# Attention feeding a four-expert layer on one core: units of queries cut to the chunks, the last chunk's tokens in a row, and one early product

## The chip, the cores and the metric

The kernel runs on one core of a Trainium2 chip. The metric is device time in microseconds (us), and lower is better. In three runs before the change it took 488.66, 488.98 and 489.07 us; the median, 488.98 us, is the time before.

A core has five engines that run their own instruction streams and wait for each other through semaphores: TensorE (PE in the profile, with its weight loads shown apart as PEld), VectorE (DVE), ScalarE (ACT), GpSimd (POOL) and SyncE (SP), which here only issues transfers.

## What is computed

Two blocks in a row. The first is attention whose weights are products of two small projections; the second sends every token through four experts and adds their outputs with normalised weights. Cut to what matters:

```
q, k, v: (4 batches, 4 heads, 1088 tokens, 32)     S1, S2: (8, 32)
phi(x)[i, j] = (S1 x)[i] * (S2 x)[j]               # 64 numbers for each token and head
kv = sum over tokens of phi(k) v^T                 # over all 1088 tokens of a batch and head
z  = sum over tokens of phi(k)
x  = (phi(q) kv) / (phi(q) z + 1e-6)               # token by token
x  -> (4352 tokens, 128)                           # batch, token; head and dim
p  = domain_probs / (sum + 1e-9)                   # (4352, 4)
out = sum over e of p[:, e] * (relu(x w1[e]) w2[e])    # w1: (4, 128, 1024), w2: (4, 1024, 128)
```

Everything is in float32. A token's output depends on the keys and values of its whole batch but on its own query only, so queries can be taken in any order.

## The kernel before

**Chunks and steps.** The expert layer is the bulk of the work. Its 4352 token columns are cut into 11 chunks (`CHUNKS`, line 67): 128, 448, 512, five of 512, 320, 256 and 128. `START` (line 69) has the first column of each. A chunk runs in 16 steps, four for each expert; a step takes 256 of the 1024 hidden features. `first` makes the step's hidden values: TensorE multiplies `xT` (tokens as columns) by `w1` into a PSUM bank named `h`, of which there are three, ScalarE applies relu (line 807), and VectorE makes the rectified differences that a fast form of the second product needs (line 778). `second` multiplies them into the output banks `o0` and `o1`. The loop at the end issues `first(i)` and then `second(i - LA)` with LA = 2, so that the two steps between hide ScalarE and VectorE. Every matmul goes through `on_side` (line 194), alternating between two halves of TensorE; `both` calls it twice. At the end of an expert `gather` copies the banks (ScalarE) and adds them with the token weights (GpSimd).

The first and the last chunk are `plain`: 128 columns, one `h` bank for a step, tokens on partitions in the output, and no differences. For the first three steps of chunk 0 the first 64 columns are multiplied ahead (`begun_hp`, `half_columns`), because half of `xT` is ready earlier than the other.

**Attention in pieces.** Attention runs inside the steps of the expert layer. `front` yields it in pieces, each with an instruction or a few: for batches 1 to 3 first `keys` (19 pieces, of which 3 turn the keys, 3 project them, 8 are products on VectorE, and two sums on TensorE), then `queries` for each unit of queries (20 pieces; the first of all has 18). A unit is a run of query columns; `UNITS` (line 65) gives the three units of each batch. The last piece of a unit sends its result through DRAM into `xT` and raises `have`. Batch 0's keys and first unit are written out in `start`.

**Pacing.** `needed` (lines 955 to 962) holds, for each chunk, how many pieces must be done for its last column, which is the count at the end of the unit that contains that column. At every step the loop takes, over all later chunks, the largest ratio of (pieces needed + 8 - pieces done) to columns left until the chunk starts, times the columns of a step; that is `rate`, pieces per step. `work`, called twice in a step, adds half of it to a credit and runs a piece for each whole credit. In the first two steps of chunk 1 nothing is added.

**The order of tokens.** VectorE turns 32 x 32 blocks, and the columns of a batch are laid so that a row of `qn` holds 34 neighbouring tokens (G = 34) of one head. So a column stands for every 34th token, and the last chunk of 128 columns holds 32 groups of 4 tokens, 34 apart. Its token weights (`ends`, line 149) and its output (line 851) follow that pattern: 32 rows of 4 x 128 numbers, 2 KB each, while the tile `end` has 128 partitions of 512 bytes.

**The start.** `start` (lines 666 and on) is one dependent chain: keys of batch 0, their products `kp` (line 383, shared between VectorE and GpSimd), the sums on TensorE (`f`), `key_divide` (`kvz`, line 406), the first 128 queries, and then chunk 0.

Of the kernel before, what the change touches and what calls it, by code (L numbers as in the profile page):

```python
# [23 lines left out]
def kernel(  # L24
# [20 lines left out]

    nc = tc.nc

    P = 128  # L50
# [11 lines left out]
    CW = 512  # L62
    GE = 160
    LA = 2
    UNITS = [[P, 448, 512]] + [[384, 384, 320]] * 2 + [[384, 320, 384]]

    CHUNKS = [P, 448, 512] + [512] * 5 + [320, 256, P]
    NC = len(CHUNKS)
# [14 lines left out]
    def psum(pool, tag):  # L83
        return pool.tile([P, 512], F32, tag=tag, name=tag)


    def load_rows(src, b, name, part=slice(0, S)):

        d = kn if name == "kn" else qn
        if b not in d:  # L90
            d[b] = lpool.tile([P, S], F32, tag=name, bufs=2, name=name)
        c, n = part.start, part.stop - part.start
        nc.sync.dma_start(d[b][:, part], bass.AP(src.tensor, src.offset + b * H * S * D + c, [[G * D, P], [1, n]]))  # L93

    def load_v(b):
        t = lpool.tile([P, H * NT * D], F32, tag="vn", name="vn")
# [29 lines left out]
    def load_w2(e):  # L126
# [14 lines left out]
    e_sum = cpool.tile([P, 2, 3], F32, name="e_sum")  # L141
    load_rows(q, 0, "qn", slice(P, S))
    load_w1(0)
    nc.sync.dma_start(
        dp.rearrange("p g e -> p (g e)"), bass.AP(domain_probs.tensor, domain_probs.offset, [[G * E, P], [1, G * E]])
    )
    for i, t in enumerate((0, (B - 1) * S + G - 4)):
        nc.sync.dma_start(
            ends[:, i, :], bass.AP(domain_probs.tensor, domain_probs.offset + t * E, [[G * E, 32], [1, 4 * E]])
        )  # L150
    load_w2(0)
    for e in range(1, E):
# [513 lines left out]
    def start():  # L666


        b, n = 0, UNITS[0][0]
        kf = []  # L670
        for t0 in (0, 2):
            key_turn(b, 0, t0, 2)
        for r in (1, 2):
            key_turn(b, r)
        qT = query_turn(b, 0, n)
        for gi in range(3):
            kf.append(psum(ps_h, "h"))
        value = value_copy(b)
        key_project(b, 0, kf[0])
        key_project(b, 1, kf[1])  # L680
        next(value)
        key_project(b, 2, kf[2])
        for _ in value:
            pass
        fq = [psum(ps_o, "o0"), psum(ps_o, "o1"), psum(ps_n, "num")]
        for i in range(3):
            for j in range(2):
                both(fq[i][:, 0:n], sr[:, i, j, :], qT[:, 0:n], start=(j == 0), stop=(j == 1))
        qb = apool.tile([P, QW], F32, tag="qb", name="qb")
        nc.scalar.copy(qb[:, 0:n], fq[0][:, 0:n])  # L690
        for x in range(2):
            key_product(b, 0, 4, 0, x, nc.vector, kf[0])
            key_product(b, 0, 4, 1, x, nc.gpsimd)
        for x in range(2):
            key_product(b, 4, 4, 0, x, nc.vector, kf[1])
            key_product(b, 8, 1, 0, x, nc.vector, kf[2])
        key_product(b, 4, 5, 1, 0, nc.gpsimd)
        key_product(b, 4, 4, 1, 1, nc.vector, kf[1])
        key_product(b, 8, 1, 1, 1, nc.vector, kf[2])
        kv = psum(ps_f, "f")  # L700
        for t0, n0 in ((0, 4), (4, 5)):
            for p in range(2):
                key_sum(b, p, kv, t0, n0)
        qp = query_tiles()
        for x in range(2):
            for p in range(2):
                query_product(qp, p, x, n, fq[1 + x], qb)
        for h in range(H):
            nc.gpsimd.tensor_copy(_ap(sq, 32 * h, 32, 32 * h, [[R2, 2], [1, R2]]), _ap(s_T, 0, 32, 0, [[D, 2], [1, R2]]))

        n1 = UNITS[b][1]
        qT = apool.tile([P, QW], F32, tag="qT2", name="qT2")
        turns = query_turns(b, n, n1, qT)
        next(turns)
        key_divide(b, kv)
        for _ in turns:
            pass
        first = attend_first(b, 0, n, qp)
        next(first)
        early[b, n] = psum(ps_o, "o1")  # L720
        both(early[b, n][:, 0:n1], sq[:, :], qT[:, 0:n1], start=True, stop=True)
        for _ in first:
            pass
        key_blocks(b, kv)
        gate_sums()
# [24 lines left out]
    def by_blocks(t, n, off=0):  # L750
        return _ap(t, 0, P, off, [[32, n // 32], [1, 32]])

    begun_hp = {}

    def half_columns(i, hp, c):

# [10 lines left out]
    def first(i, work):  # L767

        m, kq = steps[i]
        n, (e, f) = CHUNKS[m], divmod(kq, NP)
        w = n // 2
        hd = mpool.tile([P, 4 * CW], F32, tag="hid", bufs=4, name="hid")
        hid[i] = hd

        def rectify_and_subtract(out, src, in1):
            nc.vector.scalar_tensor_tensor(out=out, in0=src, scalar=0.0, in1=in1, op0=ALU.max, op1=ALU.subtract)  # L778

        if plain(m):  # L780
            if i in begun_hp:
                hp = begun_hp.pop(i)
                half_columns(i, hp, HP)
            else:
                hp = psum(ps_h, "h")
                for j in range(2):
                    both(
                        hp[:, n * j : n * j + n],
                        w1_sb[:, e, P * (2 * f + j) : P * (2 * f + j + 1)],
                        xT[:, START[m] : START[m] + n],  # L790
                        start=True,
                        stop=True,
                    )
            if m and kq % 2:
                nc.vector.tensor_scalar(
                    out=hd[:, 0 : 2 * n], in0=hp[:, 0 : 2 * n], scalar1=0.0, scalar2=None, op0=ALU.max
                )
            else:
                nc.scalar.activation(hd[:, 0 : 2 * n], hp[:, 0 : 2 * n], ACTF.Relu)  # L799
            work()  # L800
            work()
            return
        for j in range(2):
            hp = psum(ps_h, "h")
            c = P * (2 * f + j)
            both(hp[:, 0:n], w1_sb[:, e, c : c + P], xT[:, START[m] : START[m] + n], start=True, stop=True)
            nc.scalar.activation(hd[:, n * j : n * j + n], hp[:, 0:n], ACTF.Relu)  # L807
            if j == 0:
                rectify_and_subtract(hd[:, 4 * w : 5 * w], hp[:, w:n], hd[:, 0:w])
            else:  # L810
                rectify_and_subtract(
                    _ap(hd, 0, P, 5 * w, [[w, 2], [1, w]]),
                    _ap(hp, 0, P, w, [[0, 2], [1, w]]),
                    _ap(hd, 0, P, w, [[3 * w, 2], [1, w]]),
                )
                rectify_and_subtract(hd[:, 7 * w : 8 * w], hp[:, 0:w], hd[:, 6 * w : 7 * w])
            work()
# [3 lines left out]
    def second(i):  # L821
# [3 lines left out]
        if plain(m):  # L825

            if f == 0:
                acc[m] = psum(ps_o, f"o{e % 2}")
            for j in range(2):
                for _ in range(2):  # L830
                    on_side(
                        lambda s: acc[m][half[s], 0:DM],
                        lambda s: hd[:, n * j + HP * s : n * j + HP * s + HP],
                        lambda s: w2_sb[:, e, 2 * f + j, :],
                        start=(f == j == 0),
                        stop=(f == NP - 1 and j == 1),
                    )
            if f == NP - 1:
                p_e = ends[:, 1 if m else 0, e : e + 1]
                if e == 0:  # L840
                    total[m] = mpool.tile([P, P], F32, tag="end", name="end")
                    nc.vector.tensor_scalar(
                        out=total[m][:, :], in0=acc[m][:, 0:DM], scalar1=p_e, scalar2=None, op0=ALU.mult
                    )
                else:
                    nc.vector.scalar_tensor_tensor(  # L846
                        out=total[m][:, :], in0=acc[m][:, 0:DM], scalar=p_e, in1=total[m][:, :], op0=ALU.mult, op1=ALU.add
                    )
                if e == E - 1:
                    t = (START[m] // S) * S + START[m] % S // 32  # L850
                    nc.sync.dma_start(
                        bass.AP(out.tensor, out.offset + t * DM, [[G * DM, 32], [1, 4 * DM]]), total.pop(m)[:, :]
                    )
            return
        if f == 0:
            acc[m, e] = [psum(ps_o, "o0"), psum(ps_o, "o1")]
# [28 lines left out]
    def turn_back(m, src):  # L885
# [4 lines left out]
        for b, c, nn, at in parts(m):  # L890
            for a in range(4):
                nc.sync.dma_start(
                    bass.AP(
                        out.tensor,
                        out.offset + (b * S + c // 32) * DM + 32 * a,
                        [[G * DM, 32], [DM, nn // 32], [1, 32]],
                    ),
                    _ap(ob, 32 * a, 32, at, [[32, nn // 32], [1, 32]]),
                )
# [68 lines left out]
    for i in range(len(steps) + LA):  # L968
        if i < len(steps):
# [27 lines left out]
                load_batch(1)  # L997
            if m > 1 and kq == LA + 3 and m + 2 < NC:
                load_gate(m + 1)
        if i >= LA:  # L1000
            second(i - LA)
            mm, kk = steps[i - LA]
# [33 lines left out]
```

## Time and profile before

| | busy, us | instructions |
|---|---|---|
| PE, TensorE matmuls | 481.8 | 4543 |
| PEld, weight loads | 369.0 | 4543 |
| DVE, VectorE | 321.0 | 754 |
| ACT, ScalarE | 246.7 | 496 |
| POOL, GpSimd | 230.0 | 269 |

The profiled span is 487.2 us, the granted TensorE clock 0.999. Busy times of matmuls overlap, since two halves of the array run at once; the pace of TensorE is read from the starts of matmuls. Some rows that matter around the change:

| group | count | mean of one, ns |
|---|---|---|
| VectorE `hid`, line 778, 128x256 | 208 | 424 |
| VectorE `hid`, line 778, 128x512 | 96 | 686 |
| VectorE `hid`, line 778, 128x224 | 32 | 389 |
| VectorE `hid`, line 778, 128x448 | 16 | 616 |
| VectorE `kp`, line 383, 128x256 | 12 | 560 |
| VectorE `kp`, line 383, 128x320 | 12 | 709 |
| VectorE `kp` from `h`, line 383, 128x64 | 3 | 219 |
| VectorE `qp`, line 493, 64x384 | 24 | 793 |
| VectorE `qp`, line 493, 64x512 | 4 | 780 |

Transfers are busy for 19% of the 16 engines' time over the span, most of it in the first tenth, when the weights and the first two batches arrive.

### The profile page before, as it was taken

What the parts mean: (1) busy time and instruction counts of PE and PEld (TensorE: products, weight loads), DVE (VectorE), ACT (ScalarE), POOL (GpSimd) and SP (SyncE); (2) the same over time, 40 slices, a digit from 0 to 9 for tenths busy, and PEclk for the clock granted to TensorE, in tenths of its full rate; (3) what the DMA queues carried; (4) which work ended last, traced back from release to release, by engine and by line L of the source; (5) the groups of instructions that cost most, each with busy time, mean ns of one, the idle gap of its engine ahead of it and who ended that gap; (6) DMA issues with size and microseconds to landing.
All of it is one profiled execution on the core that took longest, in us unless ns stands there. A gap on an engine that the chain in (4) does not pass through costs nothing.

```text
span 487.2 us, 11354 instructions
## 1 busy us (share of the span) xinstructions
PE 481.8 (99%) x4543; PEld 369.0 (76%) x4543; DVE 321.0 (66%) x754; ACT 246.7 (51%) x496; POOL 230.0 (47%) x269
## 2 busy tenths in 40 slices
PE   8999999999999999999999999999999999999997
PEld 6966767677777777777777777777777777999997
DVE  6858685968776757768675674576574576665642
ACT  4354553445454634545455554545455555566751
POOL 5172653516354444425455354334555345565570
PEclk9999999999999999999999999999999999999999
DMA  8890230040103520041102200021101200120000
GB/s 238 259 299 11 90 93 2 22 116 1 35 1 100 123 53 1 1 118 24 34 1 86 50 2 2 1 86 24 34 0 56 50 1 0 45 54 4 15 3 18
DMA packets 37588, 26.25 MB, mean 54 GB/s; under 512 B 26016, under 2 KB 34592, under 8 KB 37024
## 3 DMA queue, kind: packets, MB, share of 16 engines
q1 hardware_dynamic: 37520, 25.53, 19.2%
q8 instruction: 36, 0.59, 0.5%
q14 instruction: 16, 0.13, 0.1%
q10 hardware_dynamic: 16, 0.00, 0.0%
HBM read 21.28 MB, written 4.24 MB: 52 GB/s over the span
## 4 chain that ended last, share of the span: by engine, by line
PE 95%; DVE 2%; DMA 1%; SPq 1%; issue 0%; ACT 0%; ACTq 0%
PE h L194 49%; PE o L194 40%; PE f L194 3%; PE den L194 2%; DMA vn<-in_v_dram 1%; DVE kp L383 1%; DVE hid L778 1%; SPq L99 0%; PE num L194 0%; DVE qp L493 0%; SPq L93 0%; ACT hid L807 0%; SPq L119 0%; DVE qT L480 0%; DVE end L846 0%
## 5 line engine op out<-in xcount | busy, mean ns | idle before, releaser
L194 PE MATMUL h<-xT,w_sb 128*64 128x512 f32 (+5 forms) x1432 | 299.5, 490 | 0.3 <-DVE hid L778 0.3
L778 DVE SCALAR_TENSOR_TENSOR hid<-h,hid 128x256 f32<-128x256 f32 (+6 forms) x432 | 203.8, 472 | 144.2 <-ACT hid L807 135.2
L807 ACT ACTIVATE hid<-h 128x512 f32<-128x512 f32 (+3 forms) x288 | 158.3, 550 | 193.8 <-PE h L194 154.1
L194 PE MATMUL o<-hid,w2s 128*64 128x256 f32 (+3 forms) x1152 | 222.8, 355 | 0.0
L194 PEld LDWEIGHTS h<-xT,w_sb 128*64 128x64 f32 x1432 | 148.8, 137 | 48.9 <-issue 4.1
L194 PE MATMUL o<-hid,w_sb 128*64 128x256 f32 (+3 forms) x864 | 184.1, 355 | 0.0
L194 PEld LDWEIGHTS o<-hid,w2s 128*64 128x64 f32 x1152 | 132.0, 137 | 29.4 <-issue 1.0
L922 POOL TENSOR_TENSOR ev<-yz,sh 64x256 f32<-64x256 f32 (+3 forms) x72 | 48.0, 667 | 161.7 <-ACT sh L925 159.0
L194 PEld LDWEIGHTS o<-hid,w_sb 128*64 128x64 f32 x864 | 100.8, 137 | 20.8 <-issue 2.1
L910 POOL TENSOR_TENSOR yz<-ev 128x512 f32<-128x512 f32 (+3 forms) x36 | 42.5, 1180 | 59.2 <-ACT ev L913 59.1
L922 POOL TENSOR_TENSOR ct<-ev 128x512 f32<-128x512 f32 (+3 forms) x36 | 42.0, 1167 | 2.8
L922 POOL TENSOR_TENSOR total<-total,ct 128x512 f32<-128x512 f32 (+3 forms) x27 | 32.4, 1200 | 2.1
L922 POOL TENSOR_TENSOR ct<-ct,gate 128x512 f32<-128x512 f32 (+3 forms) x27 | 32.2, 1191 | 2.1
L493 DVE TENSOR_TENSOR qp<-qa,qb 64x384 f32<-64x384 f32 (+3 forms) x44 | 31.9, 724 | 1.1
L912 ACT COPY ev<-o 128x512 f32<-128x512 f32 (+3 forms) x36 | 19.4, 538 | 12.0 <-PE o L194 11.5
L194 PE MATMUL o<-w_sb,hid 128*64 128x128 f32 x256 | 21.3, 274 | 0.0
L913 ACT COPY ev<-o 128x512 f32<-128x512 f32 (+3 forms) x36 | 19.4, 538 | 2.4 <-PE o L194 0.4
L194 PEld LDWEIGHTS o<-w_sb,hid 128*64 128x64 f32 x256 | 16.9, 137 | 1.8 <-issue 0.9
L799 ACT ACTIVATE hid<-h 128x256 f32<-128x256 f32 x24 | 8.8, 384 | 18.3 <-PE h L194 17.8
L383 DVE TENSOR_TENSOR kp<-fs 128x256 f32<-128x256 f32 (+1 forms) x24 | 15.1, 635 | 0.1
L194 PEld LDWEIGHTS den<-kvx,qp 128*64 128x64 f32 x264 | 13.1, 137 | 2.2 <-issue 0.2
L925 ACT COPY sh<-yz 64x256 f32<-64x256 f32 (+3 forms) x36 | 13.7, 379 | 1.6 <-POOL yz L910 0.8
(126 smaller groups left out, 239.3 us busy)
## 6 DMA issues: line engine op xcount, KB each, us to landing
w_sb<-in_moe_w_dram SPq DMA_DIRECT2D x8, 512.0 KB, 7.7
gate<-gates SPq DMA_DIRECT2D x4, 1024.0 KB, 4.8
kn<-in_k_dram SPq DMA_DIRECT2D x4, 544.0 KB, 4.3
vn<-in_v_dram SPq DMA_DIRECT2D x16, 128.0 KB, 4.5
gate<-gates SPq DMA_DIRECT2D x2, 896.0 KB, 4.5
qn<-in_q_dram SPq DMA_DIRECT2D x3, 544.0 KB, 5.7
xd<-y SPq DMA_DIRECT2D x26, 48.0 KB, 1.7
out_dram<-ob SPq DMA_DIRECT2D x16, 64.0 KB, 2.0
```

What stands on the lines that cost most here:

```text
L194: nc.tensor.matmul(out(s), weights(s), moving(s), **flags)
L383: eng.tensor_tensor(out=_ap(kps[b], 0, P, 256 * t0 + P * p + 64 * x, [[256, n], [32, 2], [R, 4], [1, R]]), in0=_ap(src, 0, P, off + 4 * x, ...
L493: nc.vector.tensor_tensor(out=qp[p][64 * x : 64 * x + 64, 0:n], in0=qa[64 * p : 64 * p + 64, 0:n], in1=qb[64 * p : 64 * p + 64, 0:n], op=A ...
L778: nc.vector.scalar_tensor_tensor(out=out, in0=src, scalar=0.0, in1=in1, op0=ALU.max, op1=ALU.subtract)
L799: nc.scalar.activation(hd[:, 0 : 2 * n], hp[:, 0 : 2 * n], ACTF.Relu)
L807: nc.scalar.activation(hd[:, n * j : n * j + n], hp[:, 0:n], ACTF.Relu)
L910: add = lambda out, in0, in1, op=ALU.add: nc.gpsimd.tensor_tensor(out=out, in0=in0, in1=in1, op=op)
L912: nc.scalar.copy(_ap(ev, 0, P, 0, [[2 * w, 2], [1, w]]), _ap(a0, 0, P, 0, two))
L913: nc.scalar.copy(_ap(ev, 0, P, w, [[2 * w, 2], [1, w]]), _ap(a1, 0, P, 0, two))
L922: add = lambda out, in0, in1, op=ALU.add: nc.gpsimd.tensor_tensor(out=out, in0=in0, in1=in1, op=op)
L925: nc.scalar.copy(sh[HP:P, 0:w], yz[0:HP, 0, 0:w])
```

## The change

It has five parts, and each can be read apart.

1. **Units.** Batch 1 is cut into 512, 320 and 256 query columns and batch 2 into 448, 512 and 128, so that units end where chunks end (at columns 1600, 2624 and 3136). The aim is to have attention asked for only when a chunk really needs it.
2. **Order of tokens in the last batch.** A row of `qn` holds 30 neighbouring tokens for the first 960 columns, and 4 for the last 128. Then the last chunk is tokens 960 to 1087 of the batch, in a row, and its output is one block of 128 rows. The loads of Q, of the token weights (`dp`, `ends`) and the stores follow. The keys and values of the batch stay in the old order.
3. **Fourth step's `hp`.** The product of step 3 with `w1` is issued between `first(2)` and `second(0)`, in the bank `num` of the attention, in two halves of 64 columns.
4. **One key product in `start`** goes from VectorE to GpSimd.
5. The last store takes 128 rows of 512 bytes in place of 32 rows of 2 KB; this is what part 2 is for.

```diff
-    UNITS = [[P, 448, 512]] + [[384, 384, 320]] * 2 + [[384, 320, 384]]
+    UNITS = [[P, 448, 512], [512, 320, 256], [448, 512, P], [384, 320, 384]]
...
-        nc.sync.dma_start(d[b][:, part], bass.AP(src.tensor, src.offset + b * H * S * D + c, [[G * D, P], [1, n]]))
+        base = src.offset + b * H * S * D
+        if name == "qn" and b == B - 1:
+            for c, n, t in ((0, (G - 4) * D, 0), ((G - 4) * D, 4 * D, S - P)):
+                nc.sync.dma_start(d[b][:, c : c + n], bass.AP(src.tensor, base + t * D, [[S * D, H], [n, 32], [1, n]]))
+        else:
+            nc.sync.dma_start(d[b][:, part], bass.AP(src.tensor, base + c, [[G * D, P], [1, n]]))
...
-    nc.sync.dma_start(
-        dp.rearrange("p g e -> p (g e)"), bass.AP(domain_probs.tensor, domain_probs.offset, [[G * E, P], [1, G * E]])
-    )
-    for i, t in enumerate((0, (B - 1) * S + G - 4)):
+    for p0, n, g0, m, t in ((0, 96, 0, G, 0), (96, 32, 0, G - 4, 3 * S), (96, 32, G - 4, 4, B * S - P)):
         nc.sync.dma_start(
-            ends[:, i, :], bass.AP(domain_probs.tensor, domain_probs.offset + t * E, [[G * E, 32], [1, 4 * E]])
+            _ap(dp, p0, n, g0 * E, [[1, m * E]]),
+            bass.AP(domain_probs.tensor, domain_probs.offset + t * E, [[m * E, n], [1, m * E]]),
+        )
+    for i, t, g in ((0, 0, G), (1, B * S - P, 4)):
+        nc.sync.dma_start(
+            ends[:, i, :], bass.AP(domain_probs.tensor, domain_probs.offset + t * E, [[g * E, 32], [1, 4 * E]])
         )
...
         key_product(b, 4, 5, 1, 0, nc.gpsimd)
+        key_product(b, 8, 1, 1, 1, nc.gpsimd)
         key_product(b, 4, 4, 1, 1, nc.vector, kf[1])
-        key_product(b, 8, 1, 1, 1, nc.vector, kf[2])
...
-    begun_hp = {}
+    begun_hp, made_hp = {}, {}
...
                 half_columns(i, hp, HP)
+            elif i in made_hp:
+                hp = made_hp.pop(i)
             else:
...
-                    t = (START[m] // S) * S + START[m] % S // 32
-                    nc.sync.dma_start(
-                        bass.AP(out.tensor, out.offset + t * DM, [[G * DM, 32], [1, 4 * DM]]), total.pop(m)[:, :]
-                    )
+                    t, to = (B * S - P, [[DM, P], [1, DM]]) if m else (0, [[G * DM, 32], [1, 4 * DM]])
+                    nc.sync.dma_start(bass.AP(out.tensor, out.offset + t * DM, to), total.pop(m)[:, :])
...
-                        [[G * DM, 32], [DM, nn // 32], [1, 32]],
+                        [[(G - 4 if b == B - 1 else G) * DM, 32], [DM, nn // 32], [1, 32]],
...
+        if i == LA:
+            made_hp[3] = psum(ps_n, "num")
+            for c in (0, HP):
+                half_columns(3, made_hp[3], c)
         if i >= LA:
             second(i - LA)
```

## The prediction

> **What bounds the kernel now.** I read the busy shares first, then the chain of work that ended last, then that chain in three windows, and last the timeline of the final microseconds.
>
> ```profile
> PE 481.8 (99%) x4543; PEld 369.0 (76%) x4543; DVE 321.0 (66%) x754; ACT 246.7 (51%) x496; POOL 230.0 (47%) x269
> ...
> PE 95%; DVE 2%; DMA 1%; SPq 1%; issue 0%; ACT 0%; ACTq 0%
> ```
>
> TensorE carries 95% of the chain. A busy matmul row alone would not prove it full, so I checked its pace: a 512-column step shows eight `h` matmuls in 1.72 us, 0.215 us for 512 columns, and fourteen `o` matmuls of 256 columns in 1.51 us, the same rate. Added up over all recorded matmuls at that rate, almost nothing is left over after 15 us except one hole. The change removes no matmul column, so it can only win back holes: at the start, near 70 us, and after the last matmul. First the start, from the chain in the window 0 to 36 us (start, length, engine and tile, count):
>
> ```profile
> 9.10 1.01 DVE kp L383 x4
> 10.31 0.29 DVE qp L493
> ...
> 11.24 0.36 DVE qT L480
> 11.71 0.30 DVE kvz L406
> ...
> 13.61 1.58 PE h L194 x48
> 15.20 0.66 PE o L194 x8
> 15.86 0.44 PE h L194 x8
> ```
>
> From 9.1 to 12.0 us VectorE is the chain. From 13.6 us TensorE is, with a weight load that idles 0.15 us for ScalarE's `hid` at 15.20. The window 60 to 92 us holds the hole:
>
> ```profile
> 64.02 0.19 ACT vx L334
> 64.22 0.45 ACT hid L807
> ...
> 65.74 1.20 DVE kp L383 x2
> ...
> 69.34 1.44 DVE kp L383
> 70.78 0.31 DVE hid L778
> 71.10 0.04 issue
> 71.14 0.97 PE h L194 x4
> ```
>
> ```profile
> 71.14 0.20 PEld L194 LDWEIGHTS h<-xT,w_sb 128*64 128x64 f32 x4 [1.05 <-DVE hid L778]
> ```
>
> ScalarE's three copies of V, then VectorE's key products of batch 1, stand in front of the `hid` work that frees a bank for `h`. The weight load waits 1.05 us; matmuls already loaded cover part of that, and from 70 to 72 us the matmul starts in the trace fall 0.69 us behind their rate. Elsewhere after 16 us no 2 us stretch loses over 0.2 us. The end, from the timeline:
>
> ```profile
> 482.30 1.52 PE L194 MATMUL o<-w_sb,hid 128*64 128x128 f32 x23
> ...
> 483.86 0.35 DVE L846 SCALAR_TENSOR_TENSOR end<-o,ends,end 128x128 f32<-128x128 f32 x1 [0.89 <-PE o L194]
> 484.24 0.60 SPq L851 DMA_DIRECT2D out_dram<-end  x1
> ```
>
> After the last matmul come one VectorE instruction, an issue of 0.60 us, and a transfer that nothing covers.
>
> **What the Trainium skill says.** (1) *Perfetto Trace Analysis*, "Identifying the Most-Contended Engine": matmul busy time is no measure of headroom, weight-load busy time is a better one. Here the latter is 76%; wide moving operands make the difference, and the pace above agrees that TensorE is full. (2) *TensorE: Matmul & The Clock Gate*, "Back-to-back issue gap": 134 cycles for 128 columns, about 60 for 64 or fewer. The trace has 0.436 us for eight of 128 columns, 54.5 ns each, which agrees; the 64-column ones take 1.58/48 = 33 ns, above the page's 25, so the measured 33 is used. (3) *GPSIMD Engine Reference*, "3.1 Elementwise": a two-input operation takes 1.96 times VectorE's time; the nearest pairs here (`kp`, 128x256: 624 ns on GpSimd, 419 or 560 on VectorE) give 1.1 to 1.5. (4) *DMA: Bandwidth & Descriptors*, "Why a DMA increments its semaphore by 16 and not by 1": the engines that share a transfer are the largest number up to 16 that divides both outermost sizes. The new load of the last batch's Q has 4 heads outermost, so 4 engines; no transfer of before has that form.
>
> **The change part by part.**
>
> *Pacing (the units).* Each step runs `rate` pieces of attention, `rate` being columns per step times the largest (needed + 8 - done)/(START - gone) over later chunks. Before, chunk 3 ends at column 1600, and the unit that passes it ends at 1856: needed is 97. After, a unit ends exactly at 1600: 77. With 22 pieces done, chunk 1 (28 columns a step) begins at 28 x (97+8-22)/(1088-128) = 2.42, and climbs to 2.64 since its first two steps earn no credit. After, chunk 7 binds instead: 28 x (235+8-22)/(3136-128) = 2.06. In chunk 2 it is 32 x (97+8-57)/512 = 3.0 before, and 32 x (235+8-51)/2560 = 2.4 after; from there 2.4 holds until chunk 7, where before it went 2.5, 2.5 to 3.0, 1.8, 1.75 to 2.0.
>
> Following the credits by hand, batch 1's keys (19 pieces) begin in step 8 of chunk 1 before and step 10 after. A step there gives TensorE 1.50 + 1.32 = 2.8 us. VectorE's own work in it is 2 x 389 + 616 = 1394 ns (rows of L778). Key products are 560 ns (128x256) and 709 ns (128x320), an addition 213. Before, steps 11, 12 and 13 hold 3, 2 and 3 pieces: 1.39 + 3 x 0.56 = 3.07, then 1.39 + 0.56 + 0.92 = 2.87, then 1.39 + 3 x 0.71 = 3.52. That is 1.06 us too much, behind 1.55 us of ScalarE copies: the hole. After, steps 12 to 15 hold two each: 2.37, 2.51, 2.87, 2.81. At most 0.07 too much, so the hole should close: **-0.69**, between -0.3 (a rest of it) and -0.8.
>
> Do wider units open another? A 512-column unit has nine dense pieces of 0.68 to 0.78 us. At 2.4 in 3.2 us steps (own work 2 x 424 + 686 = 1534 ns) the worst two steps ask 3.8 and 3.1 us: 0.6 behind. Before, the 384-column unit at rate 3 (products 793 ns) asked for 3.7 in two steps running, 1.07 behind, at about 109 us, and no hole is there. So 0. ScalarE's V copies now meet the `ev` copies in step 14 of chunk 3; before they met the second half of that work in chunk 5 without a hole. The matmuls of `attend` stay: 3+3+3 tiles against 4+3+2 and 4+4+1. xT of chunk 7 is due some 3.5 steps (11 us) after its last piece; the way through DRAM took 5.5 us (103.0 to 108.4). 0.
>
> *Key product to GpSimd.* VectorE loses one of 219 ns (row `kp<-h,fs` 128x64), so qp and qT move up by 0.2. kvz, now at 11.71, could not start before the key sums on TensorE end, 11.53 plus the usual 0.03: **-0.14**, at most -0.2. GpSimd takes 0.30 (row L262, 128x68, 298 ns) to 0.43 (219 x 1.96) from 9.74 to about 10.1; TensorE reaches the sums that read it near 10.9. Behind it wait the `sq` copies, done by 11.1 and read at 12.60. Hidden.
>
> *Fourth step's `hp` early.* Sixteen matmuls at 33 ns (0.53) replace eight at 54.5 (0.44): +0.09. They fill the 0.15 us in which the first output waits for `hid`: **-0.05**, between +0.1 and -0.15. The bank `num` is free: VectorE read it last at 14.21, and attention wants it at 21.7, long after ScalarE's pass of some 0.4 us at 15.7.
>
> *Last store.* Before, it cuts 128x128 into 32 rows of 2 KB; both such stores issue in 0.60 and 0.64 us. With 128 rows on both sides it is like `xT<-xd` of 128 x 512 B: 0.34 us; the nearest other value, Q's first 128 columns, is 0.43. I take 0.34: **-0.26**, at least -0.17. Packets stay 128 of 512 B, so the transfer does not change.
>
> *Loads.* Two more issues for `dp`, 0.33 to 0.43 us each, put everything behind them on SyncE's queue up to 0.8 us later. `w2` of expert 0 landed at 13.7 and is read at 15.2, now 15.6; `w1` of expert 1 had its last data at 14.5 and is read near 16.4. `ends` is late by as much, but its next reader on VectorE starts at 16.8. 0. Q of batch 3 on 4 engines: 32 rows each at the 232 ns that 3840-byte packets took is 7.4 us; it is read some 30 steps, over 90 us, later. 0. Output row pitch and the last gates: same sizes, 0.
>
> Sum: 0.69 + 0.14 + 0.05 + 0.26 = 1.14; 488.98 - 1.14 = **487.8**.
>
> **The rivals.** *The hole stays or moves*: what stood in front at 64 us were ScalarE's copies, and these remain. Against it stands that the overload was VectorE's, by 1.06. Then only start and end gain 0.45: 488.5. *The start gives it back*: the two issues delay `w1` of expert 1 by 0.8 beyond its slack; the slack of almost 2 us speaks against it: 487.84 + 0.76 = 488.6. *Slower*: if banks forgive less lag than I read from 109 us, the two 512 units, the 448 unit and two key sets cost about 0.4 each, 2.0, on top of the hole that stays: 488.5 + 2.0 = 490.5. The 1.07 us that before forgave speaks against it.
>
> **How the numbers follow.** Forecast 0.58, hole stays 0.25, start gives back 0.08, slower 0.09. Faster by over 0.2% means under 488.00; the forecast lies 0.2 below that, and what of it falls above is made up by a partly closed hole below: 0.58, 0.33, 0.09. Low end: the far ends 0.8 + 0.2 + 0.15 + 0.26 give 487.6, less 0.4 for the spread of runs (488.66 to 489.07): 487.2. High end: 488.6 plus 0.3: 488.9; above it lies the slower case.
>
> **What would show it.** The wait of the `h` weight load on VectorE near 70 us gone, no such wait elsewhere; batch 1's key products spread to 80 us; kvz near 11.57; no idle weight load before the first output; an issue of about 0.34 us for the last store. A new wait over 0.3 us of the `h` weight load on VectorE, or of the first `h` matmuls of a chunk on xT, would make the prediction wrong.

## The result, and the profile after

| | median, us | lowest to highest, us | runs |
|---|---|---|---|
| before, same comparison | 489.22 | 488.66 to 489.99 | 6 |
| after | 487.62 | 487.39 to 488.46 | 6 |

The ratio is 0.9968, 95% interval 0.9956 to 0.9981: the change takes 0.9 to 2.2 us off, 1.6 by the medians. The forecast was 1.14. The profiled spans went from 487.2 to 485.9 us, by 1.36 unrounded; what follows accounts for that difference.

On the page of after, the busy shares and the chain that ended last:

```profile
PE 481.5 (99%) x4551; PEld 362.7 (75%) x4551; DVE 320.9 (66%) x759; ACT 246.8 (51%) x496; POOL 230.0 (47%) x270
...
PE 97%; DMA 1%; DVE 1%; issue 0%; SPq 0%; ACT 0%; ACTq 0%
```

The busy figures hardly moved. The chain did: TensorE has 97% of it, VectorE and the SyncE queue lost a point each. That is how holes being closed looks on a page. The start, from after's chain in the window 0 to 36 us (start, length, engine and tile, count):

```profile
8.85 0.88 DVE kp L391 x3
...
10.86 0.45 DVE qT L488
11.34 0.30 DVE kvz L414
...
13.23 1.58 PE h L202 x48
14.81 0.47 PE num L202 x16
15.28 0.88 PE o L202 x16
16.15 0.44 PE h L202 x8
```

Three key products stand here, not four, and the outputs follow the early `num` matmuls without idling. Before, 1.10 us went into two groups of eight outputs (0.66 and 0.44); now sixteen take 0.88. The former hole, in the chain from 60 to 92 us:

```profile
66.77 1.51 PE h L202 x8
68.28 1.32 PE o L202 x13
69.60 1.50 PE h L202 x8
71.11 1.32 PE o L202 x13
```

Nothing but TensorE is left there, at its full pace. The end, from the timeline:

```profile
482.90 0.35 DVE L856 SCALAR_TENSOR_TENSOR end<-o,ends,end 128x128 f32<-128x128 f32 x1 [0.89 <-PE o L202]
483.28 0.35 SPq L861 DMA_DIRECT2D out_dram<-end  x1
```

The issue is 0.35 us instead of 0.60. But one thing is new, in the timeline from 302 to 308 us:

```profile
302.91 1.27 POOL L930 TENSOR_TENSOR total<-total,ct 128x512 f32<-128x512 f32 x1
302.92 1.60 DVE L391 TENSOR_TENSOR kp<-fs 128x320 f32<-128x320 f32 x1
...
304.45 0.41 DVE L786 SCALAR_TENSOR_TENSOR hid<-h,hid 128x256 f32<-128x256 f32 x1
...
304.92 0.20 PEld L202 LDWEIGHTS h<-xT,w_sb 128*64 128x64 f32 x4 [0.72 <-DVE hid L786]
```

A key product of batch 3 takes 1.60 us beside a GpSimd addition, `hid` comes late behind it, and the `h` weight load waits 0.72 us. It is the old hole in small, in another place.

To place the difference I took the time between the same instructions in every trace (one profiled execution of each kernel):

| stretch, us | before | after | difference |
|---|---|---|---|
| span's start to first turned keys (`kT`) | 5.21 | 4.96 | -0.25 |
| `kT` to `kvz` | 6.51 | 6.38 | -0.13 |
| first `h` of chunk 0 to 17th output matmul | 3.46 | 3.26 | -0.20 |
| 17th to 129th output matmul | 17.27 | 17.69 | +0.42 |
| 129th to 1345th (34 to 330 us) | 295.92 | 295.17 | -0.75 |
| 1345th to last output matmul | 153.36 | 153.32 | -0.04 |
| last output matmul to end | 3.67 | 3.27 | -0.40 |

From `kvz` to the first `h`, which the table leaves out, both take 1.82. The first row is when the keys landed, which varied from 4.8 to 5.2 us over all profiled kernels, also where nothing ahead of it differed. It is chance.

### The profile page after: what moved, and what is told of

It reads as the page before. It is cut to its first block, busy times and chain, and to the rows that moved or that the text cites. A ratio compares the mean times of both kernels' runs of the same rounds, so it can differ in the third digit from the quotient of the medians.

```text
span 485.9 us, 11377 instructions
## 1 busy us (share of the span) xinstructions
PE 481.5 (99%) x4551; PEld 362.7 (75%) x4551; DVE 320.9 (66%) x759; ACT 246.8 (51%) x496; POOL 230.0 (47%) x270
## 4 chain that ended last, share of the span: by engine, by line
PE 97%; DMA 1%; DVE 1%; issue 0%; SPq 0%; ACT 0%; ACTq 0%
PE h L202 50%; PE o L202 41%; PE f L202 3%; PE den L202 2%; DMA kn<-in_k_dram 1%; PE num L202 1%; DVE qp L501 0%; DVE kp L391 0%; DVE kT L328 0%; DVE qT L488 0%; SPq L125 0%; DVE end L856 0%; DVE kvz L414 0%; ACT fs L360 0%; ACT vx L337 0%
## 5 line engine op out<-in xcount | busy, mean ns | idle before, releaser
L501 DVE TENSOR_TENSOR qp<-qa,qb 64x512 f32<-64x512 f32 (+5 forms) x44 | 30.1, 685 | 1.0
L202 PE MATMUL o<-w_sb,hid 128*64 128x128 f32 x256 | 22.3, 273 | 0.0
L202 PEld LDWEIGHTS o<-w_sb,hid 128*64 128x64 f32 x256 | 18.1, 137 | 1.6 <-issue 0.9
L391 DVE TENSOR_TENSOR kp<-fs 128x256 f32<-128x256 f32 (+1 forms) x24 | 16.6, 696 | 0.1
```

What stands on the lines that cost most here:

```text
L202: nc.tensor.matmul(out(s), weights(s), moving(s), **flags)
L391: eng.tensor_tensor(out=_ap(kps[b], 0, P, 256 * t0 + P * p + 64 * x, [[256, n], [32, 2], [R, 4], [1, R]]), in0=_ap(src, 0, P, off + 4 * x, ...
L501: nc.vector.tensor_tensor(out=qp[p][64 * x : 64 * x + 64, 0:n], in0=qa[64 * p : 64 * p + 64, 0:n], in1=qb[64 * p : 64 * p + 64, 0:n], op=A ...
```

## The experiments

Each kernel was compared with the kernel before on the same chip; 1 us is 0.0020 in a ratio. The stretches between markers come from each kernel's profiled run.

**The units alone**, in the kernel before.

```
-    UNITS = [[P, 448, 512]] + [[384, 384, 320]] * 2 + [[384, 320, 384]]
+    UNITS = [[P, 448, 512], [512, 320, 256], [448, 512, P], [384, 320, 384]]
```

> The kernel before with the new units alone. Theory (the lower piece rate closes the hole near 70 us, VectorE being the one overloaded): the wait of the h weight load on VectorE near 70 us, 1.05 us in the kernel before, is gone; from the first expert output to the last, TensorE needs 0.5 to 0.8 us less than in the kernel before, and a wait of 0.7 us of the same kind may stand near 305 us, where the changed kernel has one. Time 488.4 to 488.8 if before is 489.2. Rival (the hole is ScalarE's copies of V and only moves): the wait comes back with about 1 us where the keys of batch 1 are now, 72 to 80 us, and the time is that of before.

Measured 488.14 us, ratio 0.9981 [0.9973, 0.9989]. The long stretch (129th to 1345th output) falls from 295.92 to 294.86. The hole at 71 us is gone and there is no wait at 305 us either. Of the 1.06, the hole is the 0.69 of the prediction; the rest lies in smaller losses such as those before at 55 and 137 us. The units are the largest part of the gain.

The key products are blocked no less than before (what blocks them is shown three experiments on); their group on the two pages, before and after, with the mean of one in ns behind the busy time:

```profile
L383 DVE TENSOR_TENSOR kp<-fs 128x256 f32<-128x256 f32 (+1 forms) x24 | 15.1, 635 | 0.1
L391 DVE TENSOR_TENSOR kp<-fs 128x256 f32<-128x256 f32 (+1 forms) x24 | 16.6, 696 | 0.1
```

So the new units do not close the hole by sparing the products. In after, three of batch 1 take 0.93, 1.23 and 1.09 us, but the eight are spread from 67.0 to 78.3 us, where before had them from 63.2 to 73.5. The units change the pace and move the pieces to later steps; no run parts these two.

**The units undone**, in the kernel after.

```
-    UNITS = [[P, 448, 512], [512, 320, 256], [448, 512, P], [384, 320, 384]]
+    UNITS = [[P, 448, 512]] + [[384, 384, 320]] * 2 + [[384, 320, 384]]
```

> The changed kernel with the old units. Theory: the hole near 70 us is back, about 0.7 us of TensorE's time, and the small wait near 305 us is gone; first output to last output takes 0.4 to 0.8 us more than in the changed kernel, time 0.4 to 0.8 us more. Rival (the earlier start or the early product is what removed the hole): no hole near 70 us, same time as the changed kernel.

Measured 488.77 us, ratio 0.9997 [0.9989, 1.0006]: without the units nothing that can be told from no change is left. The weight loads of this kernel from 66 to 76 us (in brackets the idle time before, and what ended it):

```profile
71.30 0.20 PEld L202 LDWEIGHTS h<-xT,w_sb 128*64 128x64 f32 x4 [1.04 <-DVE hid L786]
```

The wait is back at its old size (1.05 before), with every other edit in place, and the long stretch takes 295.89.

**The copies of V earlier**, in the kernel before: one after each projection of the keys, no longer all three in front of the products. The products and their pace stay.

```
+        value = value_copy(b)
...
+            next(value, None)
             yield
-        for _ in value_copy(b):
-            pass
```

> The kernel before, with ScalarE's three copies of V run one by one beside the key projections, a step or two earlier, and so out of the way of the relu in front of the hole. Rival (ScalarE's copies cause the hole): the 1.05 us wait of the h weight load near 71 us shrinks below 0.4. Theory (VectorE's key products cause it): the wait stays, 0.8 to 1.1 us, and the time is that of before within 0.3 us.

Measured 488.44 us, ratio 0.9988 [0.9979, 0.9997]. The wait at 71 us is gone, at the old pace, and the long stretch takes 295.51. I had held that VectorE's overload alone made the hole; that falls. Three key products still came together (the one at 68.10 us took 1.43), but the chain into them began about 1.2 us sooner and the lag ran out before it reached TensorE. A new wait took back part of it, in the weight loads from 128 to 136 us:

```profile
132.19 0.23 PEld L194 LDWEIGHTS h<-xT,w_sb 128*64 128x64 f32 x4 [0.41 <-ACT sh L925]
```

**The key products with one operand in PSUM**, in the kernel before. PSUM is the memory that TensorE writes its sums to; the other tiles lie in SBUF. ScalarE copies the finished sums back into a PSUM bank, and the product reads its first operand there. The pace and the copies of V stay; ScalarE has more to do. One addition on VectorE (0.21 us) also moves some pieces ahead.

```
+        nc.scalar.copy(
+            _ap(kf, 0, P, P if gi == 2 else 0, [[256, 2], [1, 32 * n]]),
+            _ap(fss[b], 0, P, 32 * t0, [[32 * NT, 2], [1, 32 * n]]),
+        )
...
-                    key_product(b, t0, n, p, x, nc.vector)
+                    key_product_back(b, t0, n, p, x, kf[1 if t0 else 0])
```

> The kernel before with the old units and the same pace, where ScalarE first copies the sums of the key projections back into a PSUM bank (three more copies of 0.2 to 0.4 us for a batch), so that the key products read one operand from PSUM and one from SBUF. In the kernel before, a product with both operands in SBUF took 0.42 (128x256) or 0.48 us (128x320) alone, and up to 1.44 when a GpSimd operation ran beside it; it then ended 0.28 or 0.35 us after that operation. Theory (that waiting made the overload): all products take 0.42 to 0.6 us whatever GpSimd does, and the wait of 1.05 us at 71 us is gone or below 0.3, at the old pace; 0.5 to 0.7 us less. Rival (the pace alone made it): the hole stays, as three products still fall on one step.

Measured 488.16 us, ratio 0.9984 [0.9977, 0.9990]. The groups of key products by form (count, then shortest, median and longest in ns), first of the kernel before, then of this one:

```profile
L383 DVE TENSOR_TENSOR kp<-fs x24: 414/483/1441, 63.2 to 292.9; 128x256 f32<-128x256 f32 x12, 128x320 f32<-128x320 f32 x12
```

```profile
L434 DVE TENSOR_TENSOR kp<-f,fs x12: 412/414/416, 63.2 to 285.5; 128x256 f32<-128x256 f32 x12
L434 DVE TENSOR_TENSOR kp<-den,fs x12: 479/481/482, 67.9 to 292.0; 128x320 f32<-128x320 f32 x12
```

No product is stretched any more, 412 to 416 and 479 to 482 ns, and no `h` weight load waits over 0.3 us. The long stretch falls to 295.16, by 0.76. The moved addition can have helped by 0.21 us; the product at 69.34 us alone lost 0.96 before (1.44 against 0.48). The products were therefore never 560 and 709 ns: they are 415 and 481, and the rest of those means was GpSimd's. Two lines of before's timeline, 64 to 76 us, show one case:

```profile
69.30 1.14 POOL L922 TENSOR_TENSOR total<-total,ct 128x448 f32<-128x448 f32 x1
...
69.34 1.44 DVE L383 TENSOR_TENSOR kp<-fs 128x320 f32<-128x320 f32 x1
```

The product ends 0.34 us after the addition. Its record holds the time it stood blocked. The Trainium skill states the rule that I had not used, in *SBUF — State Buffer*, "SBUF: two separate sides": a GpSimd instruction that reads SBUF and a VectorE instruction with two inputs in SBUF take a pair of ports in turn, and the second stands until the first is done. This trace and this kernel agree with it.

**The same in the kernel after**, with that edit.

> The changed kernel with the key products reading one operand from PSUM. In the changed kernel a wait of 0.72 us of the h weight load stands at 305 us, behind a product that took 1.60 us because a GpSimd addition had begun 10 ns before it; where the product came first (three other kernels with the new units) it took 0.49 and there was no wait. Theory: all products take 0.42 to 0.5 us, the wait at 305 us is gone, and from output 128 to output 1344 TensorE needs 294.8 to 294.9 us (295.17 in the changed kernel, 294.86 where the wait was missing): 0.3 us less. Rival (the wait comes from the pace or from ScalarE there, and three more copies on ScalarE make it worse): the wait stays near 0.7 us, same time or slower.

Measured 487.84 us, ratio 0.9972 [0.9960, 0.9984]. The long stretch is 294.86, as with the units alone, and the wait at 305 us is gone. This kernel in its timeline from 302 to 308 us:

```profile
303.29 1.28 POOL L953 TENSOR_TENSOR total<-total,ct 128x512 f32<-128x512 f32 x1
303.32 0.48 DVE L442 TENSOR_TENSOR kp<-den,fs 128x320 f32<-128x320 f32 x1
```

The two stand side by side and neither stretches. In time it gives nothing over after (487.62), since TensorE pauses for 0.54 us near 20.6 us in its profile; more on that below.

**The fourth step's early `hp` undone**, in the kernel after.

```
-        if i == LA:
-            made_hp[3] = psum(ps_n, "num")
-            for c in (0, HP):
-                half_columns(3, made_hp[3], c)
```

> The changed kernel without the early product of the fourth step. My prediction's reading: it is worth 0.05 us. The two traces' reading: 0.21 us between the start of the first h matmul and that of the third step's output (3.46 us before, 3.26 after). Theory now: 3.46 comes back, and a weight load idles about 0.15 us before the first output.

Measured 487.51 us, ratio 0.9973 [0.9963, 0.9984]: not to be told from after. From the first `h` to the 17th output it takes 3.45 us, against 3.26 with the edit. The weight loads of this kernel between 13 and 22.6 us show the 0.15 us before the first output again, and a wait that after does not have:

```profile
14.67 0.42 PEld L202 LDWEIGHTS o<-w_sb,hid 128*64 128x64 f32 x8 [0.15 <-ACT hid L809]
19.89 0.45 PEld L202 LDWEIGHTS h<-xT,w_sb 128*64 128x64 f32 x8 [0.43 <-issue]
```

The load at 19.89 is the first of expert 2 and begins 0.1 us after the last of the 16 pieces in which its `w1` landed (19.78; the other 15 were there by 18.47). Up to the 129th output this kernel takes 21.16 us from the first `h`, after 20.95. That the two end alike does not show the edit to be worth nothing, since this profile lacks the wait at 305 us. Its timeline shows why:

```profile
302.99 1.63 POOL L930 TENSOR_TENSOR total<-total,ct 128x512 f32<-128x512 f32 x1
302.99 0.49 DVE L391 TENSOR_TENSOR kp<-fs 128x320 f32<-128x320 f32 x1
```

Here the product went first and the addition was stretched, from 1.27 to 1.63. In after it was the other way about. The two start within 3 to 14 ns of each other in every kernel with the new units and both operands in SBUF. Nothing in this edit bears on which of them waits.

**The key product back on VectorE**, in the kernel after.

```
-        key_product(b, 8, 1, 1, 1, nc.gpsimd)
         key_product(b, 4, 4, 1, 1, nc.vector, kf[1])
+        key_product(b, 8, 1, 1, 1, nc.vector, kf[2])
```

> The changed kernel with the key product back on VectorE. kvz started at 11.71 us before and at 11.34 after, 0.37 us earlier, but the first turn of the keys started 0.25 us earlier as well (5.21 against 4.96), with nothing changed in front of it. Theory: the moved product is worth 0.12 to 0.15 us, the rest is the landing of the keys' load, which differs from run to run: from the first key turn to kvz 6.50 us here, 6.38 with the product on GpSimd. Rival: the whole 0.37 us belongs to the move, then 6.75 us.

Measured 487.95 us, ratio 0.9979 [0.9968, 0.9989]. `kT` to `kvz` takes 6.51 us, as before, against 6.38: the move is worth 0.13. The interval can't show so little; the traces do.

**The order of tokens undone**, in the kernel after: the loads of Q and of the token weights, the last store and the pitch of the output rows are those of before.

```
-                    t, to = (B * S - P, [[DM, P], [1, DM]]) if m else (0, [[G * DM, 32], [1, 4 * DM]])
-                    nc.sync.dma_start(bass.AP(out.tensor, out.offset + t * DM, to), total.pop(m)[:, :])
+                    t = (START[m] // S) * S + START[m] % S // 32
+                    nc.sync.dma_start(
+                        bass.AP(out.tensor, out.offset + t * DM, [[G * DM, 32], [1, 4 * DM]]), total.pop(m)[:, :]
+                    )
```

> The changed kernel with the old order of tokens: one load of dp, Q of batch 3 in one load, the last store in 32 rows of 2 KB. Theory for the end: from the start of the last output matmul to the end of the span 3.65 us as in the kernel before (3.67) and in the one with the new units alone (3.63), against 3.27 with the new store. Theory for the pause of TensorE near 20 us (0.27 us in the changed kernel, 0.40 with the units undone, none before): TensorE, now earlier, overtakes the fetch of its own instructions; each pause ended 1.42 to 1.44 us after the end of a 16 KB instruction packet. Then the pause is here too, 0.1 to 0.4 us. Rival (the two extra loads of dp delay weights): no pause, 17.3 us from the third step's output to the first of chunk 1, where the changed kernel needs 17.7.

Measured 487.93 us, ratio 0.9978 [0.9970, 0.9986]. The issue is 0.58 us again and the last output to the end takes 3.63, against 3.27; from its timeline, 481 to 488 us:

```profile
483.46 0.58 SPq L854 DMA_DIRECT2D out_dram<-end  x1
```

In the start, `w1` of expert 1 is issued at 8.44 us, against 9.93 in after. The pause near 20 us that I expected is not there, and from the 17th to the 129th output it takes 17.41. But TensorE began expert 2 at 19.82 us, 0.45 later than in after, so this run does not tell the two explanations apart.

**The early `hp` in full width**, in the kernel after: eight matmuls of 128 columns in place of sixteen of 64.

```
-            for c in (0, HP):
-                half_columns(3, made_hp[3], c)
+            for j in range(2):
+                both(
+                    made_hp[3][:, P * j : P * j + P], w1_sb[:, 0, P * (6 + j) : P * (7 + j)], xT[:, 0:P], start=True, stop=True
+                )
```

> The changed kernel with the early product in full width: eight matmuls of 128 columns in place of sixteen of 64. From the first h matmul to the third step's output 3.23 us (3.26 in the changed kernel). If the pause near 20 us is the instruction fetch, sixteen weight loads and matmuls fewer in front of it let TensorE reach the end of the fetched instructions 0.4 us later: the pause shrinks from 0.27 us to below 0.1, and the time falls by 0.2 us. If it is anything else that lands at a given time, it stays or grows by 0.03.

Measured 487.63 us, ratio 0.9974 [0.9963, 0.9984], as after. Its profile says nothing on the width: `w1` of expert 1 landed at 16.62 us (15.16 in after), and the weight load that needs it waited 0.41 us. Of its 16 pieces 15 were there by 14.80.

**Two loads of `dp` on ScalarE's queue.** After profiles so different in the start, I moved the two loads of 32 partitions that the new order added off SyncE's queue, once in after and once together with the PSUM operand.

```
+    load_dp(nc.sync, 0, 96, 0, G, 0)
...
+    load_dp(nc.scalar, 96, 32, 0, G - 4, 3 * S)
+    load_dp(nc.scalar, 96, 32, G - 4, 4, B * S - P)
```

> The changed kernel with the two short loads of dp issued by ScalarE in a gap of its work after 5.8 us, so that SyncE issues the weights 0.67 us earlier. In five profiles with the old token order the last packets of w2 of expert 2 ended at 19.0 to 19.4 us, in five with the new order at 19.7 to 20.1; of w2 of expert 0 at 12.9 to 13.1 and 13.1 to 14.1. Theory (SyncE's two more issues delay the weights): these ends come back to 19.0 to 19.4 and 12.9 to 13.1. Rival (the split transfers themselves are slower): they stay at 19.7 or later. The pause near 20 us, if it is TensorE's instruction fetch, may stay.

> The kernel of e10_kp_psum_after with the two short loads of dp issued by ScalarE. Theory: both gains, 0.3 us from the products and 0 to 0.3 from the start; the fastest of all, 487.1 to 487.4 where the changed kernel has 487.6. Rival: the two issues on ScalarE delay the key projections' copies, and the first h matmul starts 0.2 us or more later against the first key projection (7.6 us in the changed kernel); then it is no faster than e10.

The first measured 487.45 us, ratio 0.9977 [0.9963, 0.9990], with runs from 487.12 to 489.44; the second 488.39, ratio 0.9985 [0.9978, 0.9992]. Neither is a better kernel. In both profiles SyncE issued `w1` of expert 0 a full microsecond later, at 6.4 to 6.5 us against 5.41, after a pause on its own queue, and the weights landed later still: `w1` of expert 1 at 17.23 and at 16.87 us. The weight loads of the first of the two:

```profile
17.34 0.45 PEld L204 LDWEIGHTS h<-xT,w_sb 128*64 128x64 f32 x8 [1.40 <-issue]
```

TensorE stands 1.40 us and goes on 0.1 us after that landing. So the limit of the weights is close: in after the same data was there at 15.16 us and needed at 15.87.

## Why the forecast was right, and where its steps were not

**Pacing, -0.69 forecast.** The hole at 70 us closed, by the units and nothing else in the change: they alone take it away, and undoing them alone brings it back. The long stretch gained 0.75 in after and 1.06 with the units alone. But three steps of the argument were wrong.

*The durations.* I put in the means of 560 and 709 ns, as if a product had a price. It has 415 or 481 ns and, where it meets a GpSimd instruction, whatever is left of that one. The sum for step 13, three products in 3.52 us, came out near the truth only because the mean spread the blocking evenly; in the trace one of them took 1.44. The range of 414 to 1441 ns in one group of equal instructions was the sign that I passed over.

*"The overload was VectorE's".* It was one of three causes that had to meet: ScalarE's copies of V in front, three products in one step, and a product blocked by an addition. The new units, earlier copies, or unblocked products each closed the hole alone. My first rival (the hole stays because the copies remain) named a true part of the cause and still gave the wrong time, since taking away one part suffices.

*"No such wait elsewhere".* There is one, at 305 us, 0.72 us at the weight load, and the prediction had named this as what would make it wrong. It costs 0.31: the long stretch takes 295.17 or 295.18 with it (after, the kernels with the key product or the order undone, the full-width `hp`) and 294.86 without (units alone, early `hp` undone, PSUM operand, `dp` on ScalarE's queue). It hangs on which of two instructions that start within 14 ns of each other is served first. Each kernel was profiled once, so whether one kernel has it in some executions and not in others is not shown.

**Wide units, 0 forecast.** Held: no weight load waits over 0.3 us at a wide unit. The wait at 305 us is in batch 3, whose units are 384, 320 and 384 as before.

**Key product, -0.14 forecast.** Measured -0.13, from `kT` to `kvz`. In three profiles (order undone, PSUM operand in before, and PSUM operand with `dp` moved) this stretch was 6.88 to 6.92, since TensorE took 2.39 to 2.53 us for the key projections instead of 2.10. From the last of these to `kvz`, every kernel with the move took 3.69 to 3.71 and every one without it 3.82 to 3.83. On GpSimd the product took 0.30 us, 1.4 times its 0.22 on VectorE, the lower end of what I had allowed.

**Early `hp`, -0.05 forecast.** In its own place it is -0.20. Both terms were mis-sized: sixteen matmuls took 0.47, so they cost 0.03 more than the eight, not 0.09; and the break in the outputs that they fill was 0.22 (1.10 to 0.88), while I had read only the 0.15 in which the weight load idled. Then the stretch behind it gives back more than that. From 17.27 it went to 17.69 in after and 17.41 with the old order of tokens, and without the early `hp` the new order has 17.71. From the first `h` to the 129th output, before took 20.73, after 20.95, the two other kernels with after's start (units undone, PSUM operand) 21.07 and 21.24, and the one without the early `hp` 21.16. With one profile of each, what the edit is worth beyond its own place is not shown.

**Loads, 0 forecast.** Held in after's profile, with less to spare than I had read. `w1` of expert 1 was issued 1.1 us later (8.82, now 9.93), more than the 0.8 I had allowed, but landed at 15.16 against 15.04. The slack of almost 2 us was too large: I had read it from the last data, at 14.5. From the landing to the load that needs it, it was 1.4 before (15.04 to 16.45) and is 0.7 in after (15.16 to 15.87), as TensorE gets there sooner. In three experiments it was nothing. Two of these moved the `dp` loads. The third, with the full-width `hp`, has after's loads; there one piece of 16 came 1.8 us behind the rest, as one of `w1` of expert 2 came 1.3 behind where the early `hp` is undone. Why a single piece comes late stays open. Of the rival "the start gives it back" the outcome came true, 0.42 in after's profile, but not its cause: no weight load of after waits for `w1` of expert 1. The two loads of batch 3's Q landed 8.5 us after their issue (7.4 forecast) in four pieces, as the prediction had it for four heads, some 120 us before their first use.

What stands in after's own profile behind the 17th output is the following, in the weight loads from 17.2 to 22.6 us:

```profile
19.37 0.47 PEld L202 LDWEIGHTS h<-xT,w_sb 128*64 128x64 f32 x6
20.07 0.13 PEld L202 LDWEIGHTS h<-xT,w_sb 128*64 128x64 f32 x1 [0.24 <-issue]
```

This is a break in the middle of a step, after six loads of eight, with no semaphore to wait for. About 0.2 of the 0.42 is lost there. In the traces of after, of the one with the units undone and of after with the PSUM operand, it ends 1.43, 1.42 and 1.57 us after the last byte of a 16 KB instruction fetch (18.64, 18.99 and 19.00 us). That TensorE, now earlier, runs out of instructions is my inference; no experiment changed the fetch, and it stays open. Of the rest, 0.16 is lost at 28 us: there an output waits for a `hid` behind ScalarE's copies of `xT`, and these come 0.16 us sooner than before while TensorE comes 0.32 sooner.

**Last store, -0.26 forecast.** The issue fell by 0.25. From the last output to the end it is 0.40: I had the transfer unchanged, and that part came out 0.15 shorter. With the old order it is 3.63 again, and over all profiled kernels 3.63 to 3.67 with the old store and 3.26 to 3.28 with the new, so the store has it, not chance.

**The sum.** By its own steps the change moved the span by -0.75, -0.13, -0.20, +0.42, -0.40 and -0.04, together -1.10, and the landing of the keys put -0.25 of chance on top. The forecast of 1.14 is thus close to what the change did, but partly by luck, as errors cancel: the store and the early `hp` brought more, the start gave some back, and the wait at 305 us ate part of what the units had won. The +0.42 is the least certain of these numbers: the two other kernels with after's start have +0.55 and +0.72 there.

No kernel tried is shown to be faster than after; 487.45, 487.51 and 487.62 lie within the spread of one kernel's runs.

## What to carry to other kernels

Before using the mean of a group, read its shortest and longest: a threefold spread among equal instructions means that something else is in the number, and it pays to look at what ran beside the longest. When a hole has several works in front of it, ask of each whether taking it away alone would close the hole, and look for other places where the same works meet. And a gain at the start of a kernel counts only if what it runs into comes as much earlier, here loads and ScalarE's copies; the next 15 us of the trace show that.

## What the runs showed of the hardware

A VectorE product with both inputs in SBUF (128x320, 0.48 us alone) took 1.60 us beside one GpSimd addition in after and ended 0.35 us behind it. When VectorE got through first, it took 0.49 and the addition grew from 1.27 to 1.63. With one input in PSUM it never stretched, and neither did `hid`, whose inputs are one in PSUM and one in SBUF: 0.41 us at 303.40, in the middle of a GpSimd addition of the kernel without the early `hp`, and 0.38 to 0.43 for 128x256 in all traces. The Trainium skill (*SBUF — State Buffer*, same section) says that the first to start holds the ports. Recorded starts are too coarse to tell which that is: a product recorded 3 to 5 ns behind the addition went through in three profiles, and one 5 to 14 ns behind it was blocked in four.

The store of 128x128 numbers took 0.35 us to issue with 128 rows of 512 bytes on both sides, and 0.58 to 0.65 where 128 rows met 32 rows of 2 KB.
